# Taking v of block 0 by channel half, and grouping x and A by output half, in a fused attention and channel-mix kernel

## The chip, the cores and the metric

The kernel runs on one core of one Trainium2 chip. The metric is the device time of one execution in microseconds (us). A profile's span is some 1.8 us shorter than the time of the same execution, and only spans are compared with spans.

## The reference, cut to what matters

```python
def _attn_ref(q, k, v, tau):                     # B, N, C = 4, 6208, 256
    qn = q / (norm(q, axis=1) + 1e-6); kn = k / (norm(k, axis=1) + 1e-6)
    s = kn.transpose(0, 2, 1) @ qn / tau         # 256 x 256 for each batch
    a = exp(s - s.max(-1)); a /= a.sum(-1) + 1e-9
    return v @ a                                 # this is x
def _moe_ref(x, mu_k, mu_r, w_k, w_v, w_r):
    x_prev = x shifted by one token
    xk = mu_k * x + (1 - mu_k) * x_prev;  xr = mu_r * x + (1 - mu_r) * x_prev
    return sigmoid(xr @ w_r) * (relu(xk @ w_k) ** 2 @ w_v)
```

The tokens are worked in blocks of 512. In the first 36 us q and k of batch 0 are read and reduced to the 256 x 256 weights. Block 0 is the first to use the weights, so its way from v to xk is a chain in which everything else waits. To shorten it, this kernel uses that x is linear in v: the difference of neighbouring x is the product of the weights with the difference of neighbouring v. TensorE makes both, x from v and "A" from the difference, and xk is x plus a factor times A.

## The kernel before: the parts that matter

P is 128, S is 4, H is 256. TensorE's matmuls and transposes write into tiles of a PSUM pool here; ScalarE and VectorE copy the results out of it into SBUF tiles such as vT0. The PSUM pool of this program has eight buffers under four tags (kT_ps 3, vr_ps 2, xT_ps 2, s_ps 1). One such buffer is called a bank here. The source names no semaphore: the waits are put in when the program is built, and they can change when only the tiles change (VectorE's copy waited 0.55 us for ScalarE's in the changed kernel, and not in e1, below).

```python
def v_first():
    v_bf = st.pop((0, "v"))
    vT_ps = ps.tile([P, S, 2, P], BF16, name="vT_ps", tag="kT_ps", bufs=3)
    def turn_half(a):                            # 8 transposes in all
        for s in (2 * a, 2 * a + 1):
            for h in range(2):
                nc.tensor.transpose(vT_ps[:, s, h], v_bf[:, s, h * P:(h + 1) * P], ident)
    def take_half(a, copy):                      # L441
        copy(vT0[:, :, a * H + 1:(a + 1) * H + 1].rearrange("c h (s p) -> c s h p", s=2),
             vT_ps[:, 2 * a:2 * a + 2])
...
    def difference(a): ...                       # L473: dv = v - v one token earlier
    def product(a, ih):                          # a: token half; ih: channel half of v
        if ih == 0:
            pairs.append([ps.tile([P, 2, H], F32, name="x_ps", tag=tag, bufs=bufs) for tag, bufs in ...])
        for dh in range(2):                      # output half
            for t, src in zip(pairs[a], (vT0[...], dv[...])):                  # L481
                nc.tensor.matmul(t[:, dh], a_sb[:, 0, ih, dh * P:(dh + 1) * P], src,
                                 start=ih == 0 and dh == 0, stop=ih == 1, skip_group_check=True)
        if ih:
            for dh in (0, 1):                    # L485
                nc.scalar.copy(xT[:, dh, a * H + 1:(a + 1) * H + 1], pairs[a][0][:, dh])
def mix_first(key, a, dh):                       # L492, on VectorE
    nc.vector.scalar_tensor_tensor(st[0, key][:, dh, c], st[0, "ps"][a][1][:, dh], m, ...)
...
take_half(0, nc.scalar.copy)
turn(); keep_warm(2)                             # two idle matmuls
go = v_transpose_pe(1, nc.scalar.copy)           # v of block 1
invert_first(1)
take_half(1, nc.vector.tensor_copy)
difference(0); exp(); go(); weigh_first(0); weigh_first(1); difference(1)
for a in range(2):
    for ih in range(2): product(a, ih)
    for dh in range(2): mix_first("xk", a, dh)
```

Of the kernel before, what the change touches and what calls it, by code (L numbers as in the profile page):

```python
# [18 lines left out]
def kernel(  # L19
# [13 lines left out]
    nc = tc.nc  # L33
# [3 lines left out]
    P = 128  # L37
    M = 512
    S = M // P
# [12 lines left out]
    ps = ctx.enter_context(tc.tile_pool(name="ps", bufs=1, space=bass.MemoryType.PSUM))  # L52
# [8 lines left out]
    vT0 = const.tile([P, 2, M + 1], BF16, name="vT0")  # L61
# [9 lines left out]
    a_sb = const.tile([P, B, 2, C], BF16, name="a_sb")  # L71
# [313 lines left out]
    H = M // 2  # L385
# [3 lines left out]
    st = {}  # L389
# [40 lines left out]
# [5 lines that stand above are left out]
        def turn_half(a):  # L435
            for s in (2 * a, 2 * a + 1):
                for h in range(2):
                    nc.tensor.transpose(vT_ps[:, s, h], v_bf[:, s, h * P:(h + 1) * P], ident)

        def take_half(a, copy):  # L440
            copy(vT0[:, :, a * H + 1:(a + 1) * H + 1].rearrange("c h (s p) -> c s h p", s=2),  # L441
                 vT_ps[:, 2 * a:2 * a + 2])
        return turn_half, take_half

    def x_half(i, dh):
# [17 lines left out]
    def x_first():  # L463

        mix_tiles(0)
        xT = p2.tile([P, 2, M + 1], BF16, name="xT", tag="xT", bufs=3)
        st[0, "x"] = xT
        dv = st[0, "d"]
        pairs = st[0, "ps"] = []

        def difference(a):
            c = slice(a * H, (a + 1) * H)
            nc.vector.tensor_tensor(dv[:, :, c], vT0[:, :, a * H + 1:(a + 1) * H + 1], vT0[:, :, c], op=OP.subtract)  # L473

        def product(a, ih):
            if ih == 0:
                pairs.append([ps.tile([P, 2, H], F32, name="x_ps", tag=tag, bufs=bufs)
                              for tag, bufs in ((("vr_ps", 2), ("vr_ps", 2)), (("s_ps", 1), ("xT_ps", 2)))[a]])
            for dh in range(2):
                for t, src in zip(pairs[a], (vT0[:, ih, a * H + 1:(a + 1) * H + 1], dv[:, ih, a * H:(a + 1) * H])):  # L480
                    nc.tensor.matmul(t[:, dh], a_sb[:, 0, ih, dh * P:(dh + 1) * P], src,  # L481
                                     start=ih == 0 and dh == 0, stop=ih == 1, skip_group_check=True)
            if ih:
                for dh in (0, 1):
                    nc.scalar.copy(xT[:, dh, a * H + 1:(a + 1) * H + 1], pairs[a][0][:, dh])  # L485
        return difference, product

    def mix_first(key, a, dh):

        c = slice(a * H, (a + 1) * H)  # L490
        m = less[:, dh:dh + 1] if key == "xk" else less[:, 2 + dh:3 + dh]
        nc.vector.scalar_tensor_tensor(st[0, key][:, dh, c], st[0, "ps"][a][1][:, dh], m,  # L492
                                       st[0, "x"][:, dh, a * H + 1:(a + 1) * H + 1], op0=OP.mult, op1=OP.add)

    def up_first(fh, a):
# [34 lines left out]
    def mix_tiles(i):  # L530
        st[i, "d"] = p2.tile([P, 2, M], BF16, name="delta", tag="delta", bufs=2)
        st[i, "xk"] = p2.tile([P, 2, M], BF16, name="xk", tag="xk", bufs=3)
        st[i, "xr"] = p2.tile([P, 2, M], BF16, name="xr", tag="xr", bufs=3)
# [202 lines left out]
    turn_half, take_half = v_first()  # L736
# [16 lines left out]
    for a in range(2):  # L753
        for ih in range(2):
            product(a, ih)
        for dh in range(2):
            mix_first("xk", a, dh)
# [7 lines left out]
    for i in range(-2, NBLK - 1):  # L765
        for j in range(8):
# [34 lines left out]
            if 0 < i + 2 < NBLK:  # L801
                n = i + 2
# [10 lines left out]
            if j in (0, 2) and i == -1:  # L813
                for a in range(2):
                    mix_first("xr", a, int(j > 0))
            elif j in (0, 2) and 0 <= i + 1 < NBLK:
                mix(i + 1, "xr", int(j > 0))
# [67 lines left out]
```

## Time and profile before

| | before |
|---|---|
| time, median of the first 3 runs | 504.47 us (503.75 to 504.55) |
| span of the profiled run | 502.2 us |
| TensorE busy | 478.7 us, 95% |
| ScalarE's copy of v starts (L441) | 37.69 us |
| VectorE's copy of v starts (L441) | 38.31 us |
| VectorE's first mix starts (L492) | 41.12 us |
| TensorE reaches x of block 1 (L459) in the chain | 42.54 us |

The last rows are times from the start of the span, from the timeline and the chain of waits, which the prediction shows.

### The profile page before, as it was taken

How to read it: one execution, taken by the hardware profiler on the slowest of the kernel's cores; microseconds unless marked ns; L12 is line 12 of the kernel's file. 1: busy time of each engine (PE TensorE's matmuls, PEld its weight loads, DVE VectorE, ACT ScalarE, POOL GpSimd, SP SyncE). 2: the span in 40 equal slices, each digit the busy share in tenths (PEclk: the TensorE clock that was granted, in tenths of full speed). 3: DMA queues.
4: the chain of work that ended last, by engine and by line, in shares of the span. 5: the costliest groups of instructions: out<-in, count | busy, mean ns of one | idle time of the engine just before them, and what ended most of it. 6: DMA issues, size and time to landing. Idle time of an engine off the chain costs nothing.

```text
span 502.2 us, 9243 instructions
## 1 busy us (share of the span) xinstructions
PE 478.7 (95%) x3378; PEld 331.0 (66%) x3437; DVE 428.6 (85%) x786; ACT 429.0 (85%) x872; POOL 96.7 (19%) x142
## 2 busy tenths in 40 slices
PE   1789999999999999999999999999999999999996
PEld 0355677677666666767776676676666666666675
DVE  2778899999988998998989899899898787878794
ACT  3789998999899889889998898998888888788884
POOL 0044421222333132121223323100031010000000
PEclk9999999999999999999999999999999999999999
DMA  8999999999799999997599999972296757254123
GB/s 322 418 318 199 198 191 155 229 216 194 149 178 192 198 172 174 149 194 123 137 186 161 181 180 179 177 141 64 74 199 99 156 88 157 75 108 84 58 69 106
DMA packets 131542, 83.46 MB, mean 166 GB/s; under 512 B 50532, under 2 KB 125608, under 8 KB 130472
## 3 DMA queue, kind: packets, MB, share of 16 engines
q0 software_dynamic: 55824, 33.01, 50.0%
q1 hardware_dynamic: 75352, 49.59, 40.9%
q8 instruction: 27, 0.44, 0.4%
q10 hardware_dynamic: 320, 0.26, 0.2%
q14 instruction: 19, 0.16, 0.1%
HBM read 78.71 MB, written 25.43 MB: 207 GB/s over the span
## 4 chain that ended last, share of the span: by engine, by line
PE 91%; DMA 4%; ACT 2%; issue 1%; DVE 1%; SPq 0%; ACTq 0%; DVEq 0%
PE vr_ps L597 33%; PE kT_ps L565 31%; PE vr_ps L593 10%; PE xT_ps L459 8%; PE s_ps L293 6%; DMA f<-in_k_dram 4%; ACT k L160 1%; PE s_ps L199 1%; ACT qk L155 1%; PE y_ps L637 0%; PE st_ps L353 0%; ACT L735 0%; PE vT_ps L419 0%; PE x_ps L481 0%; PE kT_ps L505 0%
## 5 line engine op out<-in xcount | busy, mean ns | idle before, releaser
L570 ACT ACTIVATE kr<-kT_ps 128x512 bf16<-128x512 f32 (+1 forms) x390 | 235.0, 605 | 32.9 <-PE kT_ps L565 29.3
L597 PE MATMUL vr_ps<-w_v_sb,kk 128*128 128x256 bf16 x1536 | 230.2, 273 | 0.0
L565 PE MATMUL kT_ps<-xk,w_k_sb 128*128 128x512 bf16 (+1 forms) x722 | 217.3, 377 | 0.0
L597 PEld LDWEIGHTS <-kk 128*128 128x128 bf16 x1536 | 150.3, 98 | 57.3
L578 DVE TENSOR_TENSOR kk<-kr 128x2048 bf16<-128x2048 bf16 (+1 forms) x148 | 125.9, 852 | 0.2 <-ACT kr L570 0.2
L607 DVE SCALAR_TENSOR_TENSOR res<-res,vr_ps 128x256 f32<-128x256 f32 x192 | 80.2, 418 | 50.0 <-ACT res L606 50.0
L565 PEld LDWEIGHTS <-w_k_sb 128*128 128x128 bf16 x780 | 75.5, 98 | 27.5 <-issue 0.6
L606 ACT ACTIVATE res<-vr_ps 128x256 f32<-128x256 f32 x192 | 76.7, 400 | 1.3 <-PE vr_ps L597 1.3
L593 PE MATMUL vr_ps<-w_r_sb,xr 128*128 128x256 bf16 x384 | 73.3, 273 | 3.0
L461 ACT CAST xT<-xT_ps 128x512 bf16<-128x512 f32 x94 | 56.0, 595 | 19.9 <-PE xT_ps L459 19.6
L550 DVE SCALAR_TENSOR_TENSOR xk<-delta,mu_t,xT 128x512 bf16<-128x512 bf16 x94 | 70.1, 747 | 0.0
L550 DVE SCALAR_TENSOR_TENSOR xr<-delta,mu_t,xT 128x512 bf16<-128x512 bf16 x94 | 70.1, 747 | 0.0
L593 PEld LDWEIGHTS <-xr 128*128 128x128 bf16 x384 | 37.6, 98 | 44.6 <-issue 0.2
L133 POOL DMA_DIRECT2D qk<-in_q_dram x39 | 26.1, 670 | 167.8 <-ACT kr L570 138.2
L459 PE MATMUL xT_ps<-vT,a_sb 128*128 128x512 bf16 x188 | 55.9, 379 | 0.0
L293 PE MATMUL s_ps<-qk 128*128 128x256 bf16 (+1 forms) x294 | 55.8, 273 | 0.0
L402 POOL DMA_DIRECT2D v_bf<-in_v_dram x48 | 36.8, 767 | 97.9 <-DMA vT<-v_bf 49.3
L254 ACT ACTIVATE sq<-qk 128x1024 bf16<-128x1024 bf16 x48 | 51.1, 1065 | 0.0
L199 PE MATMUL s_ps<-qk 128*128 128x384 bf16 (+2 forms) x98 | 20.4, 359 | 14.9 <-ACT qk L155 14.9
L540 DVE TENSOR_TENSOR delta<-xT 128x1024 bf16<-128x1024 bf16 x47 | 32.3, 686 | 0.7 <-ACT xT L461 0.7
L293 PEld LDWEIGHTS <-qk 128*128 128x128 bf16 (+1 forms) x294 | 28.5, 98 | 5.6 <-issue 0.8
L133 POOL DMA_DIRECT2D qk<-in_k_dram x39 | 25.9, 665 | 3.8 <-DMA w_k_sb<-in_moe_w_k_dram 2.4
(113 smaller groups left out, 249.9 us busy)
## 6 DMA issues: line engine op xcount, KB each, us to landing
out_dram<-res SPq DMA_DIRECT2D x47, 512.0 KB, 4.8
v_bf<-in_v_dram POOLq DMA_DIRECT2D x48, 256.0 KB, 7.5
qk<-in_q_dram POOLq DMA_DIRECT2D x36, 256.0 KB, 6.1
qk<-in_k_dram POOLq DMA_DIRECT2D x36, 256.0 KB, 7.6
f<-in_q_dram SPq DMA_DIRECT2D x4, 1024.0 KB, 13.6
f<-in_k_dram SPq DMA_DIRECT2D x4, 1024.0 KB, 11.0
f<-in_q_dram SPq DMA_DIRECT2D x3, 512.0 KB, 7.7
f<-in_k_dram SPq DMA_DIRECT2D x3, 512.0 KB, 6.1
```

Of the source, the lines that this page charges most:

```text
L133: nc.gpsimd.dma_start(rows_at(qk, b, g, i)[:rows, :n], qk_src(t, b, g))
L293: nc.tensor.matmul(s_ps[:, ih, :], rows_at(qk, b, g, 0)[:rows, s, ih * P:(ih + 1) * P], rows_at(qk, b, g, 1)[:rows, s, :], start=t0 and ih ...
L459: nc.tensor.matmul(xT_ps, a_sb[:, b, ih, dh * P:(dh + 1) * P], vT[:, :, ih, :], start=ih == 0, stop=ih == 1)
L461: nc.scalar.copy(xT[:, dh, 1:], xT_ps)
L550: nc.vector.scalar_tensor_tensor(o[:, dh], st[i, "d"][:, dh], mu[:, dh:dh + 1], st[i, "x"][:, dh, :M], op0=OP.mult, op1=OP.add)
L565: nc.tensor.matmul(kT_ps[:, :m], w_k_sb[:, dh, fh * P:(fh + 1) * P], xk[:, dh, :m], start=dh == 0, stop=dh == 1)
L570: nc.scalar.activation(kr, kT_ps[:, :m], AF.Relu, scale=0.5 ** 0.5)
L578: nc.vector.tensor_tensor(st[i, "kk"][:, fh // 4 * 4 + lo:fh + 1, :m], kr, kr, op=OP.mult)
L593: nc.tensor.matmul(vr_ps[:, D:], xr[:, dh, s * P:(s + 1) * P], w_r_sb[:, dh, :], start=dh == 0, stop=dh == 1)
L597: nc.tensor.matmul(vr_ps[:, :D], kk[:, fh, s * P:(s + 1) * P], w_v_sb[:, fh, :], start=fh == 0, stop=fh == 7)
L606: nc.scalar.activation(res[:, s], vr_ps[:, D:], AF.Tanh, scale=0.5)
L607: nc.vector.scalar_tensor_tensor(res[:, s], res[:, s], 1.0, vr_ps[:, :D], op0=OP.add, op1=OP.mult)
```

## The change

The intent is to have ScalarE and VectorE take v out of PSUM at the same time, and to have x and A of one output half complete one matmul sooner. No instruction is added or removed.

```diff
-        def take_half(a, copy):
-            copy(vT0[:, :, a * H + 1:(a + 1) * H + 1].rearrange("c h (s p) -> c s h p", s=2),
-                 vT_ps[:, 2 * a:2 * a + 2])
+        def take_half(h, copy):
+            copy(vT0[:, h, 1:].rearrange("c (s p) -> c s p", s=S), vT_ps[:, :, h])
...
-            for dh in range(2):
-                for t, src in zip(pairs[a], (vT0[:, ih, ...], dv[:, ih, a * H:(a + 1) * H])):
-                    nc.tensor.matmul(t[:, dh], a_sb[:, 0, ih, dh * P:(dh + 1) * P], src,
-                                     start=ih == 0 and dh == 0, stop=ih == 1, skip_group_check=True)
-            if ih:
-                for dh in (0, 1):
-                    nc.scalar.copy(xT[:, dh, a * H + 1:(a + 1) * H + 1], pairs[a][0][:, dh])
+            for dh, t in enumerate(pairs[a]):
+                for n, src in enumerate((vT0[:, ih, c], dv[:, ih, a * H:(a + 1) * H])):
+                    nc.tensor.matmul(t[:, n], a_sb[:, 0, ih, dh * P:(dh + 1) * P], src,
+                                     start=ih == 0 and n == 0, stop=ih == 1, skip_group_check=True)
+                if ih:
+                    nc.scalar.copy(xT[:, dh, c], t[:, 0])
...
-        nc.vector.scalar_tensor_tensor(st[0, key][:, dh, c], st[0, "ps"][a][1][:, dh], m,
+        nc.vector.scalar_tensor_tensor(st[0, key][:, dh, c], st[0, "ps"][a][dh][:, 1], m,
```

More of the change, by code (lines that the diff above doesn't have):

```diff
@@ L475, in product @@
         def product(a, ih):
+            c = slice(a * H + 1, (a + 1) * H + 1)
             if ih == 0:
@@ L478, in product @@
                               for tag, bufs in ((("vr_ps", 2), ("vr_ps", 2)), (("s_ps", 1), ("xT_ps", 2)))[a]])
-            for dh in range(2):
-                for t, src in zip(pairs[a], (vT0[:, ih, a * H + 1:(a + 1) * H + 1], dv[:, ih, a * H:(a + 1) * H])):
-                    nc.tensor.matmul(t[:, dh], a_sb[:, 0, ih, dh * P:(dh + 1) * P], src,
-                                     start=ih == 0 and dh == 0, stop=ih == 1, skip_group_check=True)
-            if ih:
-                for dh in (0, 1):
-                    nc.scalar.copy(xT[:, dh, a * H + 1:(a + 1) * H + 1], pairs[a][0][:, dh])
+            for dh, t in enumerate(pairs[a]):
[4 more added lines that the diff above has]
+                    nc.scalar.copy(xT[:, dh, c], t[:, 0])
         return difference, product
```

## The prediction

> **What bounds the kernel now.** I began with the page. Its first part gives each engine's busy share, and the clock row in part 2 says whether TensorE ran slow.
>
> ```profile
> PE 478.7 (95%) x3378; PEld 331.0 (66%) x3437; DVE 428.6 (85%) x786; ACT 429.0 (85%) x872; POOL 96.7 (19%) x142
> ...
> PEclk9999999999999999999999999999999999999999
> ...
> PE 91%; DMA 4%; ACT 2%; issue 1%; DVE 1%; SPq 0%; ACTq 0%; DVEq 0%
> ```
>
> TensorE (PE) is busy 95% of 502.2 us at full clock, and the chain that ended last lies on it for 91%. The other 9% is nearly all in the first 46 us, and the change touches only block 0, which is there. So I read the chain of waits in order of time from 36 us on (columns: start us, length us, what held the chain):
>
> ```profile
> 36.27 1.28 ACT L735
> 37.56 0.01 issue
> 37.57 0.21 ACT gate L735
> 37.77 0.51 ACT vT L441
> 38.28 0.02 issue
> 38.31 0.44 DVE vT L441
> 38.74 0.02 issue
> 38.77 0.43 DVE delta L473
> 39.20 0.08 DVE sm L373
> 39.28 0.02 issue
> 39.30 0.36 DVE a_sb L374
> 39.67 0.05 issue
> 39.72 0.97 PE x_ps L481 x7
> 40.69 0.02 issue
> 40.71 0.39 ACT xT L485
> 41.10 0.02 issue
> 41.12 0.89 DVE xk L492 x2
> ```
>
> This is the part that the change edits: ScalarE takes one half of transposed v (L441), then VectorE takes the other, makes the first difference (L473) and weighs A (L374). Then come seven of the first eight matmuls of L481, ScalarE's copy of x and VectorE's two mixes. From 42.05 us (first wait for the second mix) the chain is TensorE alone, matmul behind matmul. So only what shortens 37.77 to 42.05 can move the end, and only if no wait behind it gives the time back. The timeline of that stretch shows two things the chain hides:
>
> ```profile
> 38.31 0.43 DVE L441 COPY vT<-vT_ps 128x512 bf16<-128x512 bf16 x1 [0.35 <-ACT vT L441]
> ...
> 41.71 0.11 PEld L505 LDWEIGHTS <-w_k_sb 128*128 128x128 bf16 x2 [0.33 <-DMA w_k_sb<-in_moe_w_k_dram]
> ...
> 46.15 0.59 PEld L419 LDWEIGHTS <-v_bf 128*128 128x128 bf16 x8 [0.17 <-DMA v_bf<-in_v_dram]
> ```
>
> In the first row VectorE stood 0.35 us until ScalarE's copy ended: that is the wait that the change aims at. The other rows are weight loads held by transfers, at 41.71 us for w_k and at 46.15 us for v of block 2. They are walls: earlier arithmetic does not move them.
>
> [...] All of transposed v of block 0 is 128 x 1024 bf16, 2 KiB a partition[...]. The trace agrees with an order being kept: VectorE's copy starts 0.03 us after ScalarE's ends (38.28 to 38.31). [...] VectorE's half lay partly at odd element offsets and now begins at an even one. But the trace has 426 ns for 512 elements and, at L424, 684 ns for 1024 in aligned tiles: 258 ns per 512, or 0.50 ns each. That leaves 168 ns of fixed cost, so the copy ran at that rate already; I expect 426 ns again. [...] the L481 starts 40.17, 40.30, 40.40, 40.51 lie about 0.11 apart, though each lasts 273 ns.
>
> **The change, part by part.** No instruction is added or removed on any compute engine; the orders of the two built programs match but for shapes and semaphore waits.
>
> *Take of v.* Before, each engine took a token half, two channel halves of 256 columns; now each takes one channel half, 512 columns in a row. Both moved 512 elements and still do: ScalarE 589 ns, VectorE 426 ns. The target ranges no longer interleave in vT0, so the wait could have gone on that account. But in the built program of the changed kernel VectorE's copy still waits for the same count of ScalarE's semaphore, the one that this copy of ScalarE posts, and carries no wait of its own for TensorE. The reason is the shared bank. So "at once" does not happen. ScalarE's copy waited before, and waits now, for all eight transposes, and was anyway held by its table load until 37.7 us. Sum of this part: 0.00 us.
>
> *Grouping of x and A.* Before, one bank held x of both output halves and the other A of both. ScalarE's first x copy waited for the whole x bank, written last by the 7th of the 8 matmuls. Now one bank holds x and A of output half 0, complete after the 6th. The built program says the same: the wait count falls by one for the first copy, and rises by one for the second (8th matmul). The 6th starts at 40.30 and lasts 0.27, so it ends at 40.57 instead of about 40.67 for the 7th: 0.10 to 0.11 us. The first mix starts at 41.01 instead of 41.12. The second copy waits for the 8th, about 40.78 by the row's 40.51 start and 0.27; behind the first copy it starts then at about 40.84 and ends near 41.23 (one is 0.39), before VectorE asks for it at 41.45. The mix needs ScalarE's copy as an input anyway, so x and A sharing a bank adds no wait there. Both mixes shift by 0.11, and the second-channel-half matmul of L505 goes from 42.05 to 41.94. Sum: -0.11 us at 42 us.
>
> *Walls behind it.* The first L505 matmul is held to 41.72 by w_k. The second, which carries the chain, waits for the later mix and stays behind that wall: 41.94 is after 41.72 + 0.11. So w_k takes nothing. Then TensorE runs unbroken to the v transpose of block 2 at 46.31, whose weight load v released at 46.15. TensorE already loses 0.05 us there. Come 0.11 earlier, it waits 0.16 us, if v lands at the same time; its load was issued at 36.25 us, ahead of everything that the change moves. So of the 0.11 us, 0 to 0.11 us reaches the end: all of it only if v lands early enough. Half is my estimate: -0.05 us.
>
> **Rivals.** (a) *The copies do overlap.* If the wait were gone, VectorE would start its copy after its reciprocal at 37.96 instead of 38.31. The differences and A would come up to 0.35 us earlier; the exponential of ScalarE (read out by 38.75, next L373 possible at about 38.8) limits it to about 0.3. With 0.11 that is 0.4 us at 42 us, where w_k's 41.72 would now hold, and then v's 46.15. For it speaks the intent and the disjoint targets; against it the wait in the built program and the one bank. Worth at most 0.4 us, 0.1%. (b) *A new wait replaces the old one.* Banks are freed in another order: the s_ps bank of the second token half held only x, done at 42.24, and now holds also A of output half 0, read by VectorE's xr mixes until about 43.6. The next user, the covariance matmuls of L293, starts at 45.45, so 1.8 us of room remain. The other bank is freed by the same last mix as before. Against it, then; if it bit, it would cost tenths of a us. (c) *Transfers hide everything.* If v of block 2 lands a few tenths later in a run, as a transfer of 9.9 us from issue to landing may, both kernels wait for it and the difference is 0.00. That is the likeliest rival, and it is in my half. (d) *A later phase tips.* TensorE is the bound for 450 us, each block fed by buffers well ahead; a 0.1 us shift should not change a steady rhythm. I see nothing that makes it lose 10 us.
>
> **Range and chances.** The three runs before are 503.75, 504.47 and 504.55: mean 504.26, spread 0.80. The effect of -0.05 us is a sixteenth of that spread. I take 504.3 us, between the mean and the median, less next to nothing. For the range I take that spread about it, 503.5 to 505.1, which covers v landing early or late by some tenths. To be 2% faster would take 10 us, more than the whole stretch of 37.77 to 42.05 lasts, and 2% slower would need a stall or a lower clock of which nothing here speaks: 0.01 each, 0.98 for the same.
>
> **What would show it.** In the profile after: VectorE's L441 copy still begins some 0.03 us after ScalarE's ends, with a wait near 0.35 us laid to it, and lasts about 426 ns; if they overlap, rival (a) is right. The chain shows six L481 matmuls ahead of ScalarE's x copy, not seven, and about 0.86 us there instead of 0.97. The first kT matmul is still released by w_k. The weight load of v of block 2 waits longer than 0.17 us if that wall stands; if it waits less and the chain past 47 us lies 0.1 earlier, the gain passed through. TensorE stays at 95% and about 478.7 us busy. I would be wrong if a new wait appeared on TensorE after 42 us, for the s_ps bank or a transfer, or if the clock row fell.

The sum stands as 0.00 us for the take and -0.11 us for the grouping, of which half, -0.05 us, was estimated to reach the end, so 504.3 us. The shared bank as the reason of the wait is supposition; e1 and e8 test it below (VectorE starts 0.29 and 0.17 us after ScalarE with two banks, 0.62 us with one). The 168 ns of fixed cost is an estimate, from the 426 ns and the 684 ns beside it.

## The result, and the profile after

The changed kernel took 504.15 us, median of 4 runs (503.58 to 504.52), beside 504.41 us of the kernel before (4 runs, 503.75 to 504.55). The ratio is 0.9997, with a 95% interval of 0.9979 to 1.0014: the same. A ratio here is the mean time of one kernel's fast runs over that of the other's of the same rounds, so it is not quite the ratio of the medians.

All line numbers after L470 are one lower in the changed kernel (L481 stays the matmul). From the chain of waits after (start us, length us, what held the chain):

```profile
31.99 5.05 DMA v_bf<-in_v_dram
...
37.75 0.60 ACT vT L441
...
38.37 0.44 DVE vT L441
...
39.78 0.87 PE x_ps L481 x6
...
40.66 0.39 ACT xT L484
...
41.08 0.89 DVE xk L491 x2
...
42.00 0.49 PE kT_ps L504 x3
```

The two copies still stand one behind the other, 0.02 us apart. Six matmuls instead of seven precede ScalarE's copy of x, 0.87 us instead of 0.97. The head (all that comes before this stretch) ended a little later than before, because here v of block 0 landed last (the first row) and not the table load: VectorE's copy starts at 38.37, 0.06 us later. In spite of that the first mix starts 0.04 us earlier, and TensorE goes on at 42.00 instead of 42.05. From the timeline after, the rows that the prediction pointed to:

```profile
38.37 0.43 DVE L441 COPY vT<-vT_ps 128x512 bf16<-128x512 bf16 x1 [0.55 <-ACT vT L441]
...
41.58 0.13 PEld L504 LDWEIGHTS <-w_k_sb 128*128 128x128 bf16 x2
...
46.05 0.65 PEld L419 LDWEIGHTS <-v_bf 128*128 128x128 bf16 x8
```

VectorE still waits for ScalarE, for 0.55 us, and its copy is as long as before. The other two rows have no wait in brackets: in this run neither w_k nor v of block 2 held TensorE. The page counts TensorE as 481.3 us busy, against 478.7, but it also counts 3437 matmuls against 3378: records were missing from the trace before, so those two busy times can't be compared.

### The profile page after: what moved, and what is told of

It reads as the page before. It is cut to its first block, busy times and chain, and to the rows that moved or that the text cites. A ratio compares the mean times of both kernels' runs of the same rounds, so it can differ in the third digit from the quotient of the medians.

```text
span 502.1 us, 9301 instructions
## 1 busy us (share of the span) xinstructions
PE 481.3 (96%) x3437; PEld 331.0 (66%) x3437; DVE 428.4 (85%) x786; ACT 428.7 (85%) x872; POOL 96.6 (19%) x142
## 4 chain that ended last, share of the span: by engine, by line
PE 91%; DMA 4%; ACT 2%; DVE 1%; issue 1%; SPq 1%; ACTq 0%; DVEq 0%
PE vr_ps L596 33%; PE kT_ps L564 33%; PE vr_ps L592 8%; PE xT_ps L458 8%; PE s_ps L293 6%; DMA f<-in_k_dram 3%; ACT k L160 1%; DMA v_bf<-in_v_dram 1%; SPq L125 1%; ACT qk L155 0%; PE y_ps L636 0%; PE st_ps L353 0%; DVE k L167 0%; PE kT_ps L504 0%; DVE k L170 0%
## 5 line engine op out<-in xcount | busy, mean ns | idle before, releaser
L564 PE MATMUL kT_ps<-xk,w_k_sb 128*128 128x512 bf16 (+1 forms) x780 | 229.8, 377 | 0.0
L293 PE MATMUL s_ps<-qk 128*128 128x256 bf16 (+1 forms) x294 | 55.8, 273 | 0.0
L293 PEld LDWEIGHTS <-qk 128*128 128x128 bf16 (+1 forms) x294 | 28.5, 98 | 5.6 <-issue 0.8
```

The costliest lines, as they stand in the source:

```text
L293: nc.tensor.matmul(s_ps[:, ih, :], rows_at(qk, b, g, 0)[:rows, s, ih * P:(ih + 1) * P], rows_at(qk, b, g, 1)[:rows, s, :], start=t0 and ih ...
L564: nc.tensor.matmul(kT_ps[:, :m], w_k_sb[:, dh, fh * P:(fh + 1) * P], xk[:, dh, :m], start=dh == 0, stop=dh == 1)
```

## The experiments

Ten runs were made of nine kernels, in three sets, each set with its own runs of the kernel before on the same chip. All gave correct results. Those with one run only (e2, e3, e5, e8) have the state unknown; from them I use intervals inside the trace.

### Which part did it: each alone

e3 has the new grouping and the old take; e5 has the new take and the old grouping.

```diff
 # e3, against the changed kernel
-        def take_half(h, copy):
-            copy(vT0[:, h, 1:].rearrange("c (s p) -> c s p", s=S), vT_ps[:, :, h])
+        def take_half(a, copy):
+            copy(vT0[:, :, a * H + 1:(a + 1) * H + 1].rearrange("c h (s p) -> c s h p", s=2),
+                 vT_ps[:, 2 * a:2 * a + 2])
 # e5, against the kernel before: the reverse edit
```

> Only the grouping of x and A by output half; v taken by token half as before. Theory (the grouping is the whole gain of the change): six matmuls of the first product ahead of ScalarE's copy of x, 0.87 us instead of 0.97, and from the start of VectorE's copy of v to the first mix 2.71 us as in the changed kernel, not 2.81 as before. Rival (the take has a share in it): about 2.76 or more. Time 503.6 to 504.6, not told apart by it.

> Only the take of v by channel half; x and A grouped as before, one bank. Theory (this part does nothing while both copies read one bank): VectorE's copy still begins 0.03 us after ScalarE's ends and lasts 426 ns; seven matmuls ahead of the copy of x; from VectorE's copy to the first mix 2.81 us as before. Rival (aligned target is faster): the copy takes under 400 ns. Time 503.6 to 504.6.

One row each from the chains of waits of e3 and of e5 (the same matmuls stand on L482 in e3 and on L480 in e5):

```profile
39.65 0.87 PE x_ps L482 x6
```

```profile
39.47 0.98 PE x_ps L480 x7
```

| kernel | VectorE's copy starts | first mix starts | between |
|---|---|---|---|
| before | 38.31 | 41.12 | 2.81 |
| e5, take alone | 38.06 | 40.88 | 2.82 |
| e3, grouping alone | 38.24 | 40.95 | 2.71 |
| changed (both) | 38.37 | 41.08 | 2.71 |

The grouping is the whole 0.10 us, and the take is worth nothing, as expected of both. Each row is one trace; e2 below, with the old grouping too, has 2.82 us (38.10 to 40.92). The times, 503.81 us for e3 and 503.78 us for e5, can't show it. In e5 VectorE still waited for ScalarE's copy and took 0.43 us again: the target that begins at an even element made it no faster.

```profile
38.06 0.43 DVE L441 COPY vT<-vT_ps 128x512 bf16<-128x512 bf16 x1 [0.25 <-ACT vT L441]
```

### Why the copies do not overlap: banks and targets

e1 is the changed kernel with transposed v in two PSUM banks, one per channel half. e2 is the kernel before, by token half, with one bank per token half.

```diff
 # e1
-        vT_ps = ps.tile([P, S, 2, P], BF16, name="vT_ps", tag="kT_ps", bufs=3)
+        vT_ps = [ps.tile([P, S, P], BF16, name="vT_ps", tag="kT_ps", bufs=3) for _ in range(2)]
-                    nc.tensor.transpose(vT_ps[:, s, h], v_bf[...], ident)
+                    nc.tensor.transpose(vT_ps[h][:, s], v_bf[...], ident)
-            copy(vT0[:, h, 1:].rearrange("c (s p) -> c s p", s=S), vT_ps[:, :, h])
+            copy(vT0[:, h, 1:].rearrange("c (s p) -> c s p", s=S), vT_ps[h])
 # e2: the same with two tiles [P, 2, 2, P], one for each token half
```

> The changed kernel, with transposed v of block 0 in two PSUM banks, one per channel half, so that ScalarE and VectorE no longer read one bank. Theory (the shared bank keeps the two copies in a row): VectorE's copy starts right after the transposes and its reciprocal, at about 37.85 us instead of 38.37, beside ScalarE's copy; the first difference starts near 38.3 and A is weighed about 0.3 us earlier, held then by the exponential. At the end 0.0 to 0.3 us less, because the weight loads of w_k (near 41.6) and of v of block 2 (near 46.1) become waits: about 504.0. Rival (the copies are kept in a row by something else, the target tile vT0 for one): VectorE still starts about 0.03 us after ScalarE ends, and the time is that of the changed kernel to 0.05 us.

> The kernel before, with its take by token half, and one PSUM bank per token half. Theory that the bank alone is the cause: the copies overlap as in e1. Theory that both the bank and the interleaved targets in vT0 hold them: VectorE still starts about 0.03 us after ScalarE's copy ends (near 38.3), with a wait of 0.3 to 0.5 us laid to it; the built program has that wait, so I expect this. All else as in the kernel before, 7 matmuls ahead of the copy of x, time 503.7 to 504.6.

> The kernel of e1 once more, for its trace. In e1's profile v of block 1 landed 1.1 us later and w_k 1.0 us later than in the changed kernel's, and took all of the gain. Theory (that is the scatter of transfers from run to run, and not of the kernel's making): in this run, if v of block 1 lands by about 38.4 us, A is weighed 0.3 us earlier than in the changed kernel and the first kT matmul waits for w_k near 41.6. Rival (the overlap itself delays the transfers): v of block 1 again lands at about 39.4 us.

e8 is e1 once more. The timeline of e2, then that of e8:

```profile
37.50 0.57 ACT L441 COPY vT<-vT_ps 128x512 bf16<-128x512 bf16 x1
...
38.10 0.43 DVE L441 COPY vT<-vT_ps 128x512 bf16<-128x512 bf16 x1 [0.36 <-ACT vT L441]
```

```profile
37.33 0.57 ACT L441 COPY vT<-vT_ps 128x512 bf16<-128x512 bf16 x1
...
37.50 0.41 DVE L441 COPY vT<-vT_ps 128x512 bf16<-128x512 bf16 x1
...
38.62 0.35 DVE L374 TENSOR_SCALAR a_sb<-e_sb,sm 128x256 bf16<-128x256 f32 x1
```

| | targets interleaved in vT0 (token halves) | targets apart (channel halves) |
|---|---|---|
| one bank | before: VectorE starts 0.62 us after ScalarE | changed: 0.62 us |
| two banks | e2: 0.60 us | e1: 0.29 us; e8: 0.17 us |

Only the lower right corner overlaps. It takes two things at once: the targets must not interleave in the target tile, and the sources must not share a bank. The change brought the first, and the bank kept the wait in place. In e2 it is the other way round. Why the build keeps two readers of one bank apart is not shown: no run here let them read it at once. In e2 the sources are two tiles, so what is left that both copies touch is vT0. There the two ranges interleave but hold no common element. That the build puts the wait in because it compares ranges as a whole is inferred from this; no run has interleaved targets without the wait, or a target tile for each half.

The overlap is worth 0.3 us at A: from the start of ScalarE's copy to the start of the first L374 (weighing A) it is 1.61 us before, 1.62 changed, 1.33 in e1, 1.29 in e8. But little of it arrives. In e1's profiled run v of block 1 and w_k landed late, and TensorE stood behind them. The weighed A was ready at 39.20 us, but the first matmul of x comes after the transposes of v of block 1 in the program and started at 39.92:

```profile
39.45 0.45 PEld L419 LDWEIGHTS <-v_bf 128*128 128x128 bf16 x8 [1.53 <-DMA v_bf<-in_v_dram]
...
42.51 0.33 PEld L504 LDWEIGHTS <-w_k_sb 128*128 128x128 bf16 x4 [0.96 <-DMA w_k_sb<-in_moe_w_k_dram]
```

In e8 the same kernel had v of block 1 at 38.42, but w_k still set the start of kT. From e8's chain:

```profile
33.33 8.11 DMA w_k_sb<-in_moe_w_k_dram
...
41.48 0.61 PE kT_ps L504 x4
```

So the late landing was scatter and not e1's making, since e8 did not have it: in these two runs of one kernel the weight load of v of block 1 was released at 39.45 and 38.42 us, that of w_k at 42.51 and 41.48 us. Over five rounds e1 took 503.78 us (503.47 to 504.55) against 503.79 us, ratio 0.9990, interval 0.9976 to 1.0004: not clear of noise, so the 0.0 to 0.3 us that I expected are neither confirmed nor refuted. e8's one run took 503.50 us.

### Does this stretch set the end: a known delay

e4 repeats VectorE's copy of v, to the same values, so that the chain is late by a known amount. e7 and e9 do the same with more idle matmuls ahead on TensorE.

```diff
-    take_half(1, nc.vector.tensor_copy)
+    for _ in range(6):
+        take_half(1, nc.vector.tensor_copy)
-    keep_warm(2)
+    keep_warm(14)      # e7;  keep_warm(8) in e9;  keep_warm(2) in e4
```

> The changed kernel with VectorE's copy of v done six times over (same values, right result): a known delay on the chain at 38 us, 5 x about 0.43 to 0.46 = 2.2 us. Theory (from here on the chain is one TensorE stream to the end, so what this stretch loses or gains is passed on whole, but for waits on transfers that it meets): the end comes 1.9 to 2.3 us later, 506.2 us, ratio 1.004 to the kernel before. Rival (later slack takes it in, and this stretch does not set the end at all): under 0.5 us.

> The same known delay as e4 (VectorE's copy six times), with 14 idle matmuls of 128x512 on TensorE at that place instead of 2, so that TensorE does not stand still while it waits. e4 came 3.3 us later in the profile for a delay of 2.3 us on the chain, and showed a granted clock of 0.64 from 42 to 46 us. Theory (the missing 1.0 us is TensorE's clock, lowered after its pause): clock 1.00 from 42 us on, the end 2.3 us later than the changed kernel, ratio to the kernel before about 1.0045. Rival (a lost transfer or buffer turn): still about 3.3 us, ratio 1.0067.

> As e7 with 8 idle matmuls in place of 14: in e7 two of the four timed runs came at 506.0 and 506.1, 2.3 us late, and two at 508.1 and 508.6; its profile, of a late one, has v of block 0 landing at 37.76 us, a granted clock of 0.58 from 38 to 42 us, and then the 14 idle matmuls themselves as the chain for 3.96 us. Theory (the chain passes its 2.3 us on whole; what is more is the clock after a pause of TensorE): most runs near 506.1, those with a window of lower clock later. A profile of a run near 506.1 shows clock 1.00 from 38 to 50 us; one near 507 or more shows it under 0.9 in one of the windows. Rival (something else of the delay costs the last us): runs near 507 with full clock in every window.

e4 took 507.45 us (507.21 to 508.18), ratio 1.0067, and its span of 505.4 us is 3.3 us over the changed kernel's, where I had expected at most 2.3. My expectation was wrong. A copy recurs every 0.46 us, so five more delay the chain by 2.30 us. The rest shows in a stretch of e4 (columns: stretch, its length, busy us and count of PE, weight loads, DVE, ACT and POOL; then the granted clock, DMA share, GB/s), and then the same stretch of e9:

```profile
42.00:46.00 4.00, 4.00 (x22) 2.64 (x23) 3.02 (x8) 2.26 (x7) 2.20 (x4) 0.64 1.25 200
```

```profile
42.00:46.00 4.00, 3.88 (x30) 2.65 (x29) 3.43 (x9) 2.89 (x10) 2.23 (x4) 1.00 1.27 199
```

In e4 TensorE had stood still from 39.39 to 41.95 us, with only transposes for 0.6 us before that, and its granted clock was then lower, 0.64 from 42 to 46 us. It showed only about 1.1 us after the matmuls had begun again: those of L481 start 0.11 us apart up to 42.97 and 0.21 apart from 43.25 on. Why the clock fell is not shown. The length of the pause alone did not decide it: e4's was 2.56 us, but in the profiled run of e7 one of 1.59 us (TensorE worked until 36.22) came before a clock of 0.58, and in e9 after one of 1.68 us it was 1.00. In e9 eight idle matmuls fill a part of the pause, the clock stays at 1.00, and the profiled run has a span of 504.2 us, 2.1 us over the changed kernel's. Its head had started 0.21 us earlier (VectorE's copy at 38.16), which leaves 2.09 of the 2.30 us. So the delay is passed on whole. Its five runs took 506.04 to 507.01 us, ratio 1.0049; only that of 506.04 us was profiled, so what made the later ones later is not known. e7, with 14, was a poor build: two runs came at 506.01 and 506.11 us, two at 508.12 and 508.61. In the profiled one of the late pair v of block 0 landed at 37.76 us, the clock fell to 0.58 between 38 and 42 us (the eight transposes at 37.80 took 0.94 us, against 0.62 in the changed kernel), and then the 14 idle matmuls themselves were the chain for 3.96 us:

```profile
37.80 0.94 PE L438 MATMUL vT_ps<-ident,v_bf 128*128 128x128 bf16 x8 [1.59 <-DMA v_bf<-in_v_dram]
```

The unprofiled late run, 508.61 us, had a mean granted clock of 1.0, so a lowered clock is not shown to be its cause; what it did is not known.

The spans say the same for small shifts. This is the span (to 0.01 us, as the packed traces hold it) less the time at which the chain reaches x of block 1:

| kernel | span | x of block 1 | rest |
|---|---|---|---|
| before | 502.17 | 42.54 | 459.63 |
| changed | 502.10 | 42.49 | 459.61 |
| e3 | 501.97 | 42.36 | 459.61 |
| e5 | 501.92 | 42.30 | 459.62 |
| e8 | 501.72 | 42.09 | 459.63 |
| e9 | 504.17 | 44.59 | 459.58 |

The rest is one constant to 0.05 us, so every tenth at 42 us is a tenth at the end. But kernels that should not differ there (before and e5) differ by 0.24 us: when the head starts scatters by more than the change gains.

### Could a version beat both: moving the walls

e6 is e1 with the columns of w_k that the first four matmuls need loaded first, in a tile of their own, and v of block 2 loaded ahead of w_r. e10 is e6 with the transposes and the copy of v of block 1 put after the first token half.

```diff
 # e6
-    nc.gpsimd.dma_start(w_k_sb, moe_w_k.rearrange(...)); next_load()
-    nc.gpsimd.dma_start(w_r_sb, ...); v_load(2)
+    nc.gpsimd.dma_start(w_k_a, moe_w_k[:, :2 * P].rearrange(...))
+    nc.gpsimd.dma_start(w_k_b, moe_w_k[:, 2 * P:].rearrange(...)); next_load()
+    v_load(2); nc.gpsimd.dma_start(w_r_sb, ...)
 # e10
-    go = v_transpose_pe(1, nc.scalar.copy) ... go()          # ahead of the products
+        if a == 0:
+            v_transpose_pe(1, nc.scalar.copy)()              # after product(0, 1)
```

> e1 with its walls moved: the columns of w_k that the first four matmuls need are loaded on their own ahead of the rest, and v of block 2 ahead of w_r. Theory (the overlap is worth 0.3 us, the grouping 0.1, once no transfer holds TensorE): the first kT matmul no longer waits for w_k and starts near 41.4, v's weight load at block 2 near 45.8; the end 0.3 to 0.4 us before the kernel before, ratio about 0.9993, hardly clear of noise. Rival (other transfers, v of block 0 and block 1, set the start, and their scatter is larger): ratio 0.999 to 1.001 as e1.

> e6, with the eight transposes of v of block 1 and ScalarE's copy of them moved behind the first token half's products and copies of x. In e6's profile v of block 1 landed at 38.81 us, and its transposes and ScalarE's copy (39.51 to 40.52) were the chain that held back the copy of x. Theory (v of block 1 is the next wall of the head): ScalarE's first copy of x starts at about 40.0, the first kT matmul at about 41.3 and the second, on the chain, near 41.3 to 41.4 instead of 41.77 in e6 and 42.00 in the changed kernel; the end 0.5 us before the kernel before, ratio 0.999, at the edge of noise. Rival (ScalarE's copy of v of block 1 now delays the second token half's x, or v of block 2 takes it all back at 45.8): ratio 0.9995 as e6 or worse.

e6 took 503.73 us (503.31 to 504.27) against 503.79 us, ratio 0.9995, interval 0.9981 to 1.0009. The weight load of w_k no longer waits, but from the chain of e6 the next wall is v of block 1, and behind it ScalarE's copy of it:

```profile
32.84 5.97 DMA v_bf<-in_v_dram
...
38.85 0.64 PE vT_ps L424 x8
...
39.51 1.01 ACT vT L432
40.52 0.29 ACT xT L489
```

e10 takes that off the first token half: its first kT matmul starts at 41.44 us. It then stands in front of the second half, as the chain of e10 shows:

```profile
40.77 1.01 ACT vT L432
41.78 0.29 ACT xT L489
...
42.09 0.89 DVE xk L496 x2
```

e10 took 504.00 us (503.85 to 504.44) against 503.99 us, ratio 1.0004, interval 0.9990 to 1.0018. The rival that I wrote for it is what happened. No version was shown faster than the kernel before.

## Why the prediction was right

The forecast was 504.3 us in a range of 503.5 to 505.1 and the same time; 504.15 us and a ratio of 0.9997 came. That the time fell into the range says little: the range is 1.6 us wide for an effect of 0.05 us, and a gain of nothing or of 0.3 us would have fallen into it too. What tests the prediction is the terms, one by one, in the traces.

- *The take of v is worth 0.00 us.* Right: 2.82 us with the take alone against 2.81. The reason given, the shared bank, held: with that one thing changed in e1 and e8 the copies overlap (VectorE starts 0.29 and 0.17 us after ScalarE instead of 0.62). The prediction named the interleaved targets as a possible cause too; e2 shows that they alone would have kept the wait (0.36 us there), so before the change there were two causes, and the change removed one.
- *The grouping is worth 0.10 to 0.11 us at 42 us.* Right: six matmuls instead of seven, 0.87 us, and 2.71 us instead of 2.81 to the first mix. The cost that the prediction used, 0.10 to 0.11 us, was read from the starts in the trace.
- *Walls behind it: half of the gain is lost to v of block 2.* This term was wrong, and two lines had been misread. The prediction says that TensorE already loses 0.05 us there before the change, and that 0.11 us earlier it would wait 0.16 us. The stretch before the change:

```profile
45.77 0.21 PEld L565 LDWEIGHTS <-w_k_sb 128*128 128x128 bf16 x2
...
45.88 0.38 PE L565 MATMUL kT_ps<-xk,w_k_sb 128*128 128x512 bf16 x1
...
46.31 0.61 PE L419 MATMUL vT_ps<-ident,v_bf 128*128 128x128 bf16 x8
```

Two weight loads and one matmul: the record of a matmul is missing, and the 0.05 us that the chain calls "issue" is what is left of it in the chain. From the first L293 matmul to the first transpose it is 0.86 us here (45.45 to 46.31) and 0.87 in the changed kernel, where nothing waited, so TensorE lost nothing. And the released weight load stood 0.16 us ahead of its matmul. In e8, where TensorE came earlier, the two start together:

```profile
45.91 0.45 PEld L419 LDWEIGHTS <-v_bf 128*128 128x128 bf16 x8 [0.39 <-DMA v_bf<-in_v_dram]
45.92 0.62 PE L419 MATMUL vT_ps<-ident,v_bf 128*128 128x128 bf16 x8
```

So some 0.15 us of room were left, an estimate from the 0.16 us before and the 0.01 us in e8 (the wall could come that much nearer before it held a matmul), and 0.11 us fits into it. The wait of 0.39 us of the weight load in e8 cost TensorE only 0.06 us (0.93 us for the same stretch, 44.99 to 45.92). To be expected was -0.1 us and not -0.05 us, far under the scatter either way. The other terms:

- *The first kT matmul is still released by w_k.* Wrong for the profiled run (no wait at 41.58), and of no weight, since the second one carries the chain.
- *Rival (a), that the copies overlap, would be worth at most 0.4 us.* Built in e1 and e8: 0.3 us at A, and then w_k, as the rival said. Its total at the end stays unconfirmed.
- *Rival (c), transfers that hide everything.* In another form it is the most of the story: when v of blocks 0 and 1 and w_k land moves the head by a few tenths to a full us from run to run (v of block 0 released its weight load at 36.67 us in e1, 37.09 in the changed kernel and 37.80 in e7).

## What to carry to other kernels

Before you count on two engines taking a tile at once, look in the built program for the semaphore that one waits for: here a shared PSUM bank (0.62 us from one start to the other) and interleaved targets (0.60 us) each put it there, and both had to go (0.29 and 0.17 us). The overlap was worth 0.3 us at A, and e8 then waited 0.50 us for w_k: a wait in a profile is worth what is left after the next wait behind it, so name that one first, and see whether a weight load or a matmul is what waits. Before you count an "issue" of the chain as lost time, compare the stretch with another run: a missing matmul record looked the same here (0.05 us). When you test a chain with a known delay, check the granted clock in the stretch: e4's span came 3.3 us later for a delay of 2.30 us, with a clock of 0.64, and e9's, with eight idle matmuls in the pause, 2.1 us later with 1.00. e7, with 14, had 0.58 from 38 to 42 us, after a pause of 1.59 us ahead of them.
